# Attention and feed-forward kernel on one core: one of four chains of the first product of batches 2 to 5 written as one level of Strassen

## The chip, the core and the metric

The kernel runs on one core of a Trainium2 chip. The engines of the core are TensorE (PE in the profile, with PEld for the loading of its weights), VectorE (DVE), ScalarE (ACT), GpSimd (POOL) and SyncE (SP, which here only issues DMA transfers). Each engine works through its own list of instructions in the order in which the program wrote them, and waits on semaphores for the others. The metric is device time in microseconds (us); lower is better.

## The reference, cut to what matters

For 8 batches, 12 heads, 448 rows and 64 columns a head, the reference computes attention with normed q and k, and passes the result x (8 x 448 rows, 768 columns) through two matrix products with a leaky ReLU between them:

```python
q_n, k_n = rmsnorm(q, g_q), rmsnorm(k, g_k)
scores = 1/sqrt(64) * q_n @ k_n.T ; scores -= max ; attn = exp(scores) ; attn /= sum
x = (attn @ v) laid out as (3584, 768)
h = x @ w_in              # 768 -> 2048, the first product
g = maximum(0.01 * h, h)
out = g @ w_out           # 2048 -> 768, the second product
```

## The kernel before, in words

**Units.** The attention is cut into 24 units u of four heads each; three units make a batch (`NQ` is 3). In the main loop each unit has four quarters d = 0 to 3. In each quarter TensorE first makes the scores of one or two steps of keys (`qk`, L195; one step in quarter 0, two in the others, each into a slot of two PSUM banks, of which there are two). ScalarE takes the exponential of each slot (`ex`, L214), about 1 us a slot. In quarter 0 the unit also fixes its shift: VectorE takes the maximum of the first scores (`shift_max`, L232 and L234), TensorE spreads it with a matmul (`shift_mm`, L244), VectorE reduces once more (L245) and makes the bias `eb` (L253). Between the two, TensorE runs attention times v (`pv`, L340) and the row sums (`zcol`, L283) of the unit before. ScalarE copies the former out of PSUM (L295), SP spreads the reciprocal row sums (`rz`, L310), and GpSimd multiplies the two into the fp16 tile `xt` of the batch (L320).

**Preparation.** Two units ahead, q and k are normed: ScalarE squares them (`prep_sq`, L144, quarter 3), VectorE sums the squares (`prep_ssq`, L155, quarter 1), ScalarE makes the reciprocal root with a logarithm and an exponential (`prep_rinv`, `uu` on L160 and `rinv` on L161, quarter 2, written behind the exponentials of that quarter), VectorE multiplies (`prep_norm`, L167, once for q and once for k), and a transposing DMA on SP makes `qkT` (L179), which VectorE scales (`prep_g`, L151). The q and k tiles rotate through three buffers (`raws`), and unit u issues the loads of unit u + 4 in its quarter 0.

**The filling work.** The two products of a batch are cut into items, held in the list `queue`. `push(b)` adds those of batch b in quarter 3 of the first unit of batch b + 1, and `fill` (L702) takes some of them after the scores of each quarter, by a planned cost per item, so that they are spread over three units. A batch of the middle has 16 items of the first product, one for each of 16 row tiles of 128 hidden columns, called M here (`moe1`, L358): 6 matmuls of 448 columns into one PSUM bank, then one leaky ReLU by ScalarE (`prelu`, L356) into the fp16 tile `gt`. Then come the items of the second product: plain ones (`moe2`, L403) and groups of seven (`seven`, L444), a level of Strassen, with its operand sums on VectorE (`s1` to `s4`, L425 to L434). An even batch runs `moe2` for one tile and then one `seven`; an odd one runs two `seven`. The results go through the `ost` tiles (four buffers) to HBM on SP.

**What orders the work.** The program is written out under a manual schedule: each engine's order is the order in which the functions are called. A step of an item that reads its result (a copy, an addition, a ReLU) is put off with `later` and written at the head of the next item (`flush`). The jobs of a quarter (`jobs`) are written between its items, one after each. Four PSUM banks (`aux`) serve the items in rotation. `hold` takes all four into a list kept by the program, from which `aux` then takes the first and to which `drop` gives back.

**Where Strassen stands before.** Only batches 6 and 7 use it for the first product (`late1`, L552). A chain s covers four row tiles (2s, 2s + 1, 8 + 2s, 9 + 2s), and has seven items instead of four M: each has 6 matmuls of 224 columns (L564). Its operands are sums of weights (`win_sum`, L533) and sums of x (`x_sum`, L550); VectorE copies and adds the products in PSUM (L577, L583, L612) and ScalarE applies the ReLU (L574). Batch 6 has two chains beside 8 M, batch 7 has four. The weight sums of the second half of the tiles and the x sums of batch 6 are made in quarter 0 of unit 22.

Of the kernel before, what the change touches and what calls it, by code (L numbers as in the profile page):

```python
# [8 lines left out]
FP32 = mybir.dt.float32  # L9
# [9 lines left out]
def kernel(  # L19
# [47 lines left out]
    def drop(bank):  # L67
        if held:
            held[0].append(bank)

# [45 lines left out]

    def load(u, engines=None):
        raw[u] = [raws.tile([P, 2, NS, D], FP32, tag=name, name=name) for name in ("rq", "rk")]
        st[u] = {}
        for t, src, eng in zip(raw[u], (q, k), engines or (nc.sync, nc.sync)):  # L120
            eng.dma_start(t.rearrange("p a t d -> p a (t d)"), rows(src, u))
# [12 lines left out]
    def buf(u, name):  # L134
        if name not in st[u]:
            shape, dtype, bufs = SHAPES[name]
            st[u][name] = prep_p.tile(shape, dtype, tag=name[:2] if bufs == 3 and name != "qkT" else name, bufs=bufs, name=name)
        return st[u][name]
# [219 lines left out]
    def moe1(b, ft):  # L358
        xt = xts[b]
        hps = aux([P, 512], FP32, "hps")  # L360
        for kt in range(KT):
            nc.tensor.matmul(hps[:, 0:S], win16[:, kt // 2, kt % 2, ts(ft, P)], xt[:, kt // 2, kt % 2],  # L362
                             start=(kt == 0), stop=(kt == KT - 1))
        prelu(b, gt[:, ft, 64 * (b % 2):64 * (b % 2) + S], hps[:, 0:S])
        drop(hps)
# [157 lines left out]
    def win_sum(n, x, tile_=None, eng=nc.vector):  # L523
        if tile_ is None:
            ws[n, x] = win_b(1, 0, 4 * x, 4)
        else:
            pool, tag, bufs = tile_
            ws[n, x] = pool.tile([P, HK, 512], FP16, tag=tag, bufs=bufs, name="ws")
        a, b = {1: (lambda: (win_b(1, 0, 4 * x, 4), win_b(1, 1, 4 * x, 4))),
                2: (lambda: (ws[1, x], win_b(0, 0, 4 * x, 4))),  # L530
                3: (lambda: (win_b(0, 0, 4 * x, 4), win_b(1, 0, 4 * x, 4))),
                4: (lambda: (win_b(0, 1, 4 * x, 4), ws[2, x]))}[n]()
        eng.tensor_tensor(ws[n, x], a, b, op=ALU.add if n == 1 else ALU.subtract)  # L533
# [5 lines left out]
    def x_tiles():  # L539
        if not xs:  # L540
            two = [prep_p.tile([P, 2, HK, HX], FP16, tag="sq", bufs=3, name="xs") for i in range(2)]
            for n in range(1, 5):
                xs[n] = two[n // 3][:, (n - 1) % 2].rearrange("p k (t x) -> p k t x", t=NS)

    def x_sum(b, n):
        x_tiles()
        t = xs
        a, c = {1: (x_b(b, 0, 1), x_b(b, 0, 0)), 2: (x_b(b, 1, 1), t[1]),
                3: (x_b(b, 1, 1), x_b(b, 0, 1)), 4: (x_b(b, 1, 0), t[2])}[n]
        nc.vector.tensor_tensor(t[n], a, c, op=ALU.subtract)  # L550

    def late1(b, tail, after):  # L552
# [36 lines left out]
        def start():  # L589
            hold()  # L590
            if tail:
                for i in range(2):
                    drop(slot()[:, 0])
            for name in ("u", "v"):
                if name not in tmp:
                    tmp[name] = raws.tile([P, 2, S], FP32, tag="rq" if name == "u" else "rk", name=name)

        def item(n, s):
# [11 lines left out]
            elif n == 7:  # L610
                mm(get(7, s), 7, s, xs[3], True)
                later(lambda: nc.vector.tensor_copy(tmp["v"][:, s % 2], g[7, s][:, 0:S]))  # L612
            elif n == 6:
                mm(g[1, s], 6, s, xs[2], False)
                later(lambda: vadd(g[7, s][:, 0:S], g[1, s], tmp["v"][:, s % 2]))
            elif n == 5:
                mm(g[1, s], 5, s, xs[1], False)
                later(lambda: vadd(tmp["v"][:, s % 2], g[1, s], tmp["v"][:, s % 2]))
                later(lambda: out_(s, 1, 1, tmp["v"][:, s % 2]))
            elif n == 4:  # L620
                mm(g[7, s], 4, s, xs[4], False)
                later(lambda: out_(s, 1, 0, g[7, s][:, 0:S]))
                later(lambda: drop(g[7, s]))
            else:
                mm(g[1, s], 3, s, x_b(b, 1, 1), False)
                later(lambda: out_(s, 0, 1, g[1, s][:, 0:S]))
                later(lambda: drop(g[1, s]))
            for fn in after.get((n, s), ()):
                pend.append(fn)

        return item

    LATE_ALL = ((1, 0), (2, 0), (7, 0), (1, 1), (6, 0), (7, 1), (1, 2), (5, 0), (4, 0), (6, 1), (3, 0), (2, 1), (7, 2), (5, 1),
                (4, 1), (6, 2), (3, 1), (1, 3), (7, 3), (5, 2), (4, 2), (6, 3), (3, 2), (2, 2), (5, 3), (4, 3), (2, 3), (3, 3))
    LATE_HALF = ("M", "M", "M", "M", "M", "M", (1, 2), (7, 2), (2, 2), (6, 2), "M", (1, 3), (5, 2), (4, 2), (7, 3), (3, 2), (6, 3),
# [11 lines left out]
    def push(b):  # L647
# [7 lines left out]
        if late:  # L655
# [5 lines left out]
            else:  # L661
                after[6, 2] = [lambda: win_sum(1, 0, (raws, "rq", 3))]
                after[1, 3] = [lambda: win_sum(2, 0, (raws, "rk", 3))]
                after[5, 2] = [lambda: win_sum(4, 0, (prep_p, "n16", 1))]
            item = late1(b, odd, after)
            fts = [0, 8, 1, 9, 2, 10, 3, 11]
            items = []
            for w in (LATE_ALL if odd else LATE_HALF):
                if w == "M":
                    items.append((1.13, lambda ft=fts.pop(0): (flush(), moe1(b, ft))))  # L670
                else:
                    items.append((0.575, lambda w=w: item(*w)))
        if odd:
            tt, tn = (3, 4), (5, 6)
            items += [(1.31, fn) for fn in seven(pair, tt, tn)]
            for n, x, fs in ((len(items) - 7, 1, (s3, s4)),) if late else ((8, 0, (s1, s2)), (10, 0, (s3, s4)), (FT - 1, 1, (s1, s2)), (FT, 1, (s3, s4))):
# [67 lines left out]
    with tc.manual_schedule():  # L744
# [182 lines left out]
        for u in range(3, NU):  # L927
            for d in range(4):
# [24 lines left out]
                if d == 0:  # L953
# [8 lines left out]
                    if u + 4 < NU:  # L962
                        job(load, u + 4)
# [18 lines left out]
                if u + 2 < NU:  # L982
# [3 lines left out]
                    if d == 2:  # L986
# [3 lines left out]
                        if u > 3:  # L990
                            job(prep_trd, u + 2)
                if d == 1 and 4 <= u < 8:
# [3 lines left out]
                if d == 2 and 6 <= u < 8:  # L996
                    job(xmul_sb, u - 1)
                if u == NU - 2 and d == 0:
                    for n, tile_ in ((1, (raws, "rq", 3)), (2, (raws, "rk", 3)), (3, None), (4, (prep_p, "sq", 3))):
                        job(win_sum, n, 1, tile_)  # L1000
# [45 lines left out]
```

## Time and profile before

| | |
|---|---|
| median of 3 runs | 422.35 us (421.35 to 423.44) |
| profiled execution | 422.04 us, of which the span from first to last instruction is 420.3 us |
| PE busy | 404.4 us, 96% of the span |
| ACT busy | 303.6 us, 72% |
| DVE busy | 269.2 us, 64% |
| POOL busy | 83.0 us, 20% |
| first product, 448 columns (L362) | 600 matmul records, 120.8 us busy |
| its leaky ReLU (L356) | 100 instructions, 556 ns each |

Busy is the time in which an engine had an instruction running. Matmuls overlap in the records, so one lasts longer than the distance to the next; what a matmul costs is that distance. "Idle before" an instruction is the time for which its engine waited for it, with the releaser named behind an arrow. The middle stage, batches 2 to 5 in units 9 to 20, lies between about 143 us and 340 us.

### The profile page before, as it was taken

The numbers are of one execution on the slowest core, as the hardware profiler recorded it, in microseconds if no ns is written. First come the engines' busy times: TensorE is split into PE (matmuls) and PEld (weight loads), VectorE is DVE, ScalarE is ACT, GpSimd is POOL, SyncE is SP. The second block draws the span as 40 slices with busy tenths as digits, with TensorE's granted clock in tenths as the row PEclk, the third lists the DMA queues.
The fourth block names the chain that finished last, engine by engine and source line by source line (L and its number), as shares of the span: only waits on it lengthen the run. The fifth ranks groups of instructions, "written<-read, shape, count | busy, mean of one in ns | idle before, by whom it ended". The sixth has DMA issues, their size and how long they took to land.

```text
span 420.3 us, 9568 instructions
## 1 busy us (share of the span) xinstructions
PE 404.4 (96%) x3959; PEld 222.9 (53%) x3959; DVE 269.2 (64%) x440; ACT 303.6 (72%) x474; POOL 83.0 (20%) x75
## 2 busy tenths in 40 slices
PE   7977999999999999999999999999999999999995
PEld 6544444555445544555445544455445557558853
DVE  5788665787658736466448745467338787527762
ACT  5999878868987689867986779967986657653600
POOL 1958422300020111210121111120101101010000
PEclk9699999999999999999999999999999999999999
DMA  8999999889664795678565796578562460032023
GB/s 257 218 239 237 235 250 147 200 156 215 169 153 68 224 212 120 168 163 180 152 130 107 194 203 150 151 141 170 180 111 44 121 155 11 7 78 75 2 53 100
DMA packets 71951, 62.42 MB, mean 149 GB/s; under 512 B 36324, under 2 KB 67044, under 8 KB 71908
## 3 DMA queue, kind: packets, MB, share of 16 engines
q1 hardware_dynamic: 61312, 49.62, 47.2%
q0 software_dynamic: 10272, 11.80, 18.1%
q8 instruction: 31, 0.51, 0.5%
q10 hardware_dynamic: 324, 0.39, 0.3%
q14 instruction: 12, 0.10, 0.1%
HBM read 45.61 MB, written 11.01 MB: 135 GB/s over the span
## 4 chain that ended last, share of the span: by engine, by line
PE 83%; ACT 8%; DVE 6%; issue 1%; DMA 1%; SPq 0%; DVEq 0%; ACTq 0%
PE hps L362 27%; PE sT L195 8%; PE sT L340 6%; PE ma L444 5%; PE md L444 5%; PE mc L444 5%; ACT et L214 5%; PE bank L444 5%; PE bank L564 4%; PE op L403 3%; PE zc L283 3%; PE mb L444 3%; DVE n L167 2%; PE sT L444 2%; PE bank L403 1%
## 5 line engine op out<-in xcount | busy, mean ns | idle before, releaser
L214 ACT ACTIVATE et<-sT,eb 128x896 f16<-128x896 f32 x166 | 159.4, 1010 | 18.6 <-PE sT L195 16.9
L362 PE MATMUL hps<-xt,win 128*128 128x448 f16 x600 | 120.8, 353 | 0.2 <-DVE xt L349 0.2
L362 PEld LDWEIGHTS <-win 128*128 128x128 f16 x612 | 56.8, 98 | 58.2 <-issue 9.6
L320 POOL TENSOR_TENSOR xt<-x,rz 128x896 f16<-128x896 f32 x16 | 33.4, 2085 | 148.0 <-DMA rz<-zs 139.5
L356 ACT ACTIVATE gt<-hps 128x448 f16<-128x448 f32 x100 | 54.0, 556 | 6.1 <-PE hps L362 5.4
L167 DVE TENSOR_TENSOR n<-rq,rinv 128x896 f16<-128x896 f32 (+2 forms) x25 | 27.2, 1090 | 47.0 <-ACT rinv L161 44.2
L195 PE MATMUL sT<-qkT 64*64 64x448 f16 x664 | 53.2, 369 | 3.0 <-ACT et L214 1.9
L155 DVE TENSOR_REDUCE ssq<-sq 128x14 f32<-128x896 f32 (+2 forms) x49 | 50.3, 1058 | 1.6 <-ACT sq L144 1.6
L444 PEld LDWEIGHTS <-sa 128*128 128x128 f16 x352 | 32.8, 98 | 26.3 <-issue 6.1
L295 ACT COPY x<-sT 128x896 f32<-128x896 f32 x19 | 17.2, 906 | 36.4 <-DVE sT L245 36.4
L124 POOL DMA_DIRECT2D vt<-in_v_dram x24 | 18.2, 757 | 114.9 <-PE sT L340 107.4
L444 PEld LDWEIGHTS <-gt 128*128 128x128 f16 x264 | 25.2, 98 | 18.7 <-issue 2.1
L195 PEld LDWEIGHTS <-qkT 64*64 64x64 f16 x672 | 15.2, 105 | 36.8 <-issue 33.5
L340 PE MATMUL sT<-et,vt 64*64 64x448 f16 x532 | 28.5, 350 | 0.3
L403 PE MATMUL op<-wout,gt 128*128 128x384 f16 x160 | 28.4, 327 | 0.0
L232 DVE TENSOR_REDUCE sT<-sT 128x1 f32<-128x896 f32 x22 | 24.1, 1093 | 4.3 <-PE sT L195 4.3
L340 PEld LDWEIGHTS <-vt 64*64 64x64 f16 x672 | 20.7, 107 | 11.3 <-issue 1.7
L167 DVE TENSOR_TENSOR n<-rk,rinv 128x896 f16<-128x896 f32 (+2 forms) x26 | 26.1, 1009 | 0.0
L403 PEld LDWEIGHTS <-gt 128*128 128x128 f16 x192 | 17.6, 98 | 14.3 <-issue 3.0
L444 PE MATMUL ma<-wout,gt 128*128 128x384 f16 x128 | 23.5, 326 | 0.0
L425 DVE TENSOR_TENSOR sa<-gt 128x512 f16<-128x512 f16 (+1 forms) x15 | 8.2, 544 | 18.5 <-ACT gt L356 13.9
L144 ACT ACTIVATE sq<-rq 128x896 f32<-128x896 f32 (+2 forms) x18 | 16.3, 913 | 1.3 <-DMA rq<-in_q_dram 1.3
(135 smaller groups left out, 516.6 us busy)
## 6 DMA issues: line engine op xcount, KB each, us to landing
rq<-in_q_dram SPq DMA_DIRECT2D x24, 448.0 KB, 3.9
rk<-in_k_dram SPq DMA_DIRECT2D x24, 448.0 KB, 5.6
out_dram<-ost SPq DMA_DIRECT2D x52, 192.0 KB, 3.3
rz<-zs SPq DMA_DIRECT2D x76, 112.0 KB, 2.3
vt<-in_v_dram POOLq DMA_DIRECT2D x24, 224.0 KB, 5.1
win<-in_moe_w_in_dram POOLq DMA_DIRECT2D x8, 384.0 KB, 16.8
wout<-in_moe_w_out_dram POOLq DMA_DIRECT2D x2, 1536.0 KB, 29.7
out_dram<-ost SPq DMA_DIRECT2D x4, 96.0 KB, 2.1
```

The source lines that it names most:

```text
L124: nc.gpsimd.dma_start(vts[u % NV].rearrange("p a t d -> p a (t d)"), rows(v, u))
L155: nc.vector.tensor_reduce(buf(u, "ssq")[:, ti, :, c[0]:c[1]], buf(u, f"sq{ti}")[:, :, c[0]:c[1]], axis=AXL.X, op=ALU.add)
L167: nc.vector.tensor_tensor(buf(u, "n16")[:, ti, c[0]:c[1]].rearrange("p s a d -> p a s d"), src[:, :, c[0]:c[1]], buf(u, "rinv")[:, ti, :, ...
L195: nc.tensor.matmul(banks[a][64 * r:64 * r + 64, 0:S].rearrange("p (t x) -> p t x", t=NS), kT(u, r, a, t), qT(u, r, a), start=True, stop=True)
L214: nc.scalar.activation(s["et"][:, t], sT[:, :, 0:S], AF.Exp, bias=s["eb"], scale=1.0)
L232: nc.vector.tensor_reduce(s["spare"][:, 511:512], sT[:, :, 0:S], axis=AXL.XY, op=ALU.max)
L320: eng.tensor_tensor(xts[b][:, g], s["x32"], s["rz"], op=ALU.mult)
L340: nc.tensor.matmul(s["pv"][r][64 * a:64 * a + 64, 0:S], vts[u % NV][64 * r:64 * r + 64, a, t], s["et"][64 * r:64 * r + 64, t, a], start=(t ...
L356: nc.scalar.activation(dst, src, AF.Prelu, bias=0.0, scale=1.0, alpha=0.01)
L362: nc.tensor.matmul(hps[:, 0:S], win16[:, kt // 2, kt % 2, ts(ft, P)], xt[:, kt // 2, kt % 2], start=(kt == 0), stop=(kt == KT - 1))
L403: nc.tensor.matmul(op2[:, 0:HC], gt[:, ft, ds(col(t), P)], wout16[:, ft, ds(HC * half, HC)], start=(ft == 0), stop=(ft == FT - 1))
L444: nc.tensor.matmul(bank[:, 0:HC], a[:, f], b[:, f], start=(first and f == 0), stop=(f == HF - 1), skip_group_check=not first)
```

## The change

In batches 2 to 5 the chain s = 2 (row tiles 4, 5, 12 and 13) is computed by seven Strassen items instead of four M. The other twelve tiles stay M. The list `MID_HALF` sets the order of the 19 items; each is named by product and chain.

- The items of the chain are in the new function `mid`. It takes three banks: product 1 in one, product 7 in one, and a third that first gets a copy of product 1 by VectorE and in which products 6, 5 and 3 are then accumulated. That third bank is taken by `written`, from those whose 448 columns TensorE has written. Products 2 and 4 are accumulated on 1 and 7. VectorE makes a copy of 1, a copy of 7 into an `ost` tile `w`, and two additions; ScalarE makes four ReLUs of 448 columns.
- The four x sums of a batch are written as jobs in quarter 0 of its middle unit (units 10, 13, 16 and 19), behind the maximum, into two `ost` tiles.
- The weight sums of the upper half of the tiles are halved: their first 256 columns are made in unit 9, one in each quarter, and the rest in quarter 0 of unit 22.
- Buffers: q and k tiles and squares now rotate through two buffers from unit 9 on; the third holds the weight sums. From unit 7 on the loads of unit u + 4 are written in quarter 2, behind the transposing DMA, instead of in quarter 0.
- The banks are held in the program's list from batch 2 on, instead of from batch 6.
- The first halves of the sums `s1` to `s4` of an odd batch are written at items 14 and 15 (before: 8 and 10), the second halves at 18 and 19 (before: 15 and 16).

By the built program the order on the engines moves in these places: in unit 10 the VectorE order is now square sum, copy of 1, square sum, copy of 7, norm of q, first addition, norm of k, second addition (unit 16 alike); in unit 13 it is copy of 1, square sum, copy of 7, square sum, first addition, norm of q, norm of k, second addition (unit 19 alike). In unit 11 (and 17) TensorE's quarter 2 has one M and one `moe2` item and quarter 3 two `moe2` items (before: two M and one `moe2`, then one `moe2`), and VectorE has norm of q, `s1`, norm of k, the copy of `moe2`, `s2`, `s3`, `s4` and then the maximum of the next unit (before: both norms, `s1`, copy, `s2`, maximum, with `s3` and `s4` behind the bias). In unit 13 ScalarE's ReLU of `w` stands ahead of the two exponentials of quarter 3.

```diff
-    def drop(bank):
+    full = []
+    def drop(bank, whole=False):
         if held:
             held[0].append(bank)
+            full[:] = [x for x in full if x is not bank] + [bank] * whole
+    def written():
+        for i, x in enumerate(held[0]):
+            if any(x is y for y in full):
+                return held[0].pop(i)
...
+    def ring(pool, tag, third, shape, dtype, name):
+        return pool.tile(shape, dtype, tag=tag + "ab"[third], bufs=1 if third else 2, name=name)
...
-        raw[u] = [raws.tile([P, 2, NS, D], FP32, tag=name, name=name) for name in ("rq", "rk")]
+        raw[u] = [ring(raws, name, u in (2, 5, 8), [P, 2, NS, D], FP32, name) for name in ("rq", "rk")]
...
+        def mid(n, s):
+            flush()
+            hold()
+            if n == 1:
+                mm(get(1, s), 1, s, x_b(b, 0, 0), True)
+                later(lambda: g.__setitem__((6, s), written()))
+                later(lambda: nc.vector.tensor_copy(g[6, s][:, 0:S], g[1, s][:, 0:S]))
+            elif n == 7:
+                mm(get(7, s), 7, s, xs[b][3], True)
+                g["w", s] = opool.tile([P, S], FP32, tag="ost", name="w")
+                later(lambda: nc.vector.tensor_copy(g["w", s], g[7, s][:, 0:S]))
+            elif n == 2:
+                mm(g[1, s], 2, s, x_b(b, 1, 0), False)
+                later(lambda: out_(s, 0, 0, g[1, s][:, 0:S]))
+                later(lambda: drop(g[1, s], True))
+            elif n == 6:
+                mm(g[6, s], 6, s, xs[b][2], False)
+                later(lambda: vadd(g[7, s][:, 0:S], g[6, s], g["w", s]))
+            elif n == 5:
+                mm(g[6, s], 5, s, xs[b][1], False)
+                later(lambda: vadd(g["w", s], g[6, s], g["w", s]))
+                later(lambda: out_(s, 1, 1, g["w", s]))
+            elif n == 4:
+                mm(g[7, s], 4, s, xs[b][4], False)
+                later(lambda: out_(s, 1, 0, g[7, s][:, 0:S]))
+                later(lambda: drop(g[7, s], True))
+            else:
+                mm(g[6, s], 3, s, x_b(b, 1, 1), False)
+                later(lambda: out_(s, 0, 1, g[6, s][:, 0:S]))
+                later(lambda: drop(g[6, s], True))
...
+    MID = 2
+    MID_HALF = ("M", "M", "M", (1, 2), (7, 2), "M", (2, 2), (6, 2), "M", (5, 2), (4, 2), "M", (3, 2), "M", "M", "M", "M", "M", "M")
...
-            item = late1(b, odd, after)
-            fts = [0, 8, 1, 9, 2, 10, 3, 11]
+        if b >= MID:
+            item = late1(b, late and odd, after)
+            fts = [0, 8, 1, 9, 2, 10, 3, 11, 6, 14, 7, 15]
...
-                    if u + 4 < NU:
+                    if u + 4 < NU and u < 7:
                         job(load, u + 4)
...
                         if u > 3:
                             job(prep_trd, u + 2)
+                        if u + 4 < NU and u >= 7:
+                            job(load, u + 4)
...
+                if u == 3 * MID + 3:
+                    n, tile_ = ((1, (raws, "rqb", 1)), (2, (raws, "rkb", 1)), (4, (prep_p, "sqb", 1)), (3, None))[d]
+                    job(win_sum, n, 1, tile_, 0)
+                if d == 0 and u % NQ == 1 and MID < u // NQ <= LATE:
+                    for n in (3, 1, 2, 4):
+                        job(x_sum, u // NQ - 1, n)
```

## The prediction

> **What bounds the kernel now.** I read the page's slices, then busy time by stretch, then the timelines of units 10 and 12, then the chain of waits for the rate of matmuls.
>
> ```profile
> PE   7977999999999999999999999999999999999995
> ...
> DVE  5788665787658736466448745467338787527762
> ACT  5999878868987689867986779967986657653600
> ```
>
> ```profile
> 150.00:175.00 25.00, 25.00 (x213) 11.74 (x212) 10.51 (x14) 23.32 (x41) 4.90 (x3) 1.00 0.71 169
> 200.00:225.00 25.00, 25.00 (x211) 12.29 (x210) 13.27 (x23) 21.26 (x36) 4.94 (x3) 1.00 0.55 133
> ```
>
> The columns: stretch, length, busy time of PE, PEld, DVE, ACT, POOL, then clock and DMA. TensorE has no gap in the middle stage: a matmul removed there is worth its full time, a wait put there costs its full time. VectorE is half idle, but the average does not say when it reaches an instruction. Its order does (unit 10, third quarter):
>
> ```profile
> 155.34 2.44 PE L362 MATMUL hps<-xt,win 128*128 128x448 f16 x12
> 155.39 1.90 ACT L214 ACTIVATE et<-sT,eb 128x896 f16<-128x896 f32 x2
> ...
> 157.16 0.55 ACT L356 ACTIVATE gt<-hps 128x448 f16<-128x448 f32 x1
> 157.59 0.34 ACT L160 ACTIVATE uu<-ssq,eps_t 128x28 f32<-128x28 f32 x1
> ...
> 157.96 0.23 ACT L161 ACTIVATE rinv<-uu 128x28 f32<-128x28 f32 x1
> ...
> 158.21 1.48 DVE L167 TENSOR_TENSOR n<-rq,rinv 128x896 f16<-128x896 f32 x1 [6.63 <-ACT rinv L161]
> ```
>
> VectorE stands 6.63 us before the norm of q, for a root that ScalarE makes behind two exponentials. Whatever is written on VectorE behind that norm waits too; before, nothing for TensorE stood there. And the border to unit 12, the maximum and the matmul that needs it:
>
> ```profile
> 176.04 1.52 PE L340 MATMUL sT<-et,vt 64*64 64x448 f16 x28
> ...
> 176.74 1.09 DVE L232 TENSOR_REDUCE sT<-sT 128x1 f32<-128x896 f32 x1
> ...
> 177.86 0.29 DVE L234 TENSOR_TENSOR dg<-ident,sT 128x128 f16<-128x128 f16 x1
> ...
> 178.27 0.23 PE L244 MATMUL sT<-dg,onesp 128*128 128x64 f16 x2
> ```
>
> The operand `dg` is ready at 178.15 and used at 178.27: about 0.1 us of slack.
>
> [...] in the timeline 12 of 448 columns and the step to the scores take 2.38 us (155.34 to 157.72), and in the chain of waits 12 of 224 take 1.15 us, 96 ns each. [...] in the built program products 5 and 3 do wait for VectorE.
>
> **The change part by part.** F is the time at which a quarter's filling items start, after its scores.
>
> *Matmuls.* A batch gives up 24 of 448 columns (24 x 0.1885 = 4.52 us) and gets 42 of 224 (42 x 0.096 = 4.03). Gain 0.49, four batches: **-1.97 us**, all on the path. ReLUs: four of 448 columns for four, no change.
>
> *VectorE work added.* Per batch four x sums (0.50 us each by their row, 2.0), copies and additions (0.62 each; PSUM to PSUM has no row, I bound it by 0.54, the copy of 384 columns, and 0.65, just above the PSUM addition of 0.63). The sums stand behind `eb`; the 6.63 us idle cover them and the copies. The square sums get later, but the second ends 3.6 us after the second quarter's F, 2.4 us before ScalarE asks for it. Without that cover it would be up to 2 us a batch. The weight sums (half of a 0.95 us row, about 0.5 each) are only moved; in unit 22 they stood under an M-filled quarter, so I count no gain.
>
> *First addition, units 10 and 16.* The root: 158.21 - 155.34 = 2.87 after F, minus 0.43 (157.16 to 157.59) since no ReLU stands ahead of it now: 2.44. The norm of q takes 1.01 from start to start in the undisturbed units, the addition 0.62: done at F + 4.1. Product 5 overwrites the bank that the addition reads. TensorE asks for it after products 2 and 6 (1.15), an M (1.13) and the scores (0.6): F + 2.9. Wait 1.2. Also, the second quarter's first and last item share a bank: its ReLU stands behind two exponentials, 0.1 more. Queued behind on TensorE: everything. Bounds 0.8 (short norm) to 2.1 (norm at its 1.48 us, bank wait 0.45). **2 x 1.36 = +2.7 us**.
>
> *Second addition, units 13 and 19.* Here it follows both norms: 2.45 + 1.01 + 1.0 + 0.62 = F + 5.1. Product 3 is asked for after products 6, 5, 4 (1.73), M (1.13), the scores (0.6), M (1.13): F + 4.6. Wait 0.5. And the ReLU of `w` waits for it ahead of the last two exponentials on ScalarE: ReLU, ReLU of product 4 (0.43 each), two exponentials (1.9) end at F + 7.9, where attention times v would have been reached at F + 6.6. Together 1.3; then ScalarE catches up by the next bias (its work before the copy of x adds up to 2.9 us, the bias comes at 2.9). Bounds 0.8 to 2.0. **2 x 1.3 = +2.6 us**.
>
> *The maximum of units 12 and 18.* Two `moe2` items now lie ahead of the border, so `s3` and `s4` (0.6 us each from start to start) come before the maximum, less 0.2 that the copy waited: it is 1.0 later against 0.1 of slack, while TensorE arrives as before. I take 1.0 (bounds 0.5 to 1.5): **+2.0 us**. In return the longer fourth quarter covers the exponentials for which `pv` waited there (scores end 175.77, `pv` 176.04; alike in 18): **-0.5 us**.
>
> *The border to unit 10.* One `seven` item (1.3 us) slips from unit 9 to 10. `pv` then waits 0.3 for the exponentials; the maximum, behind a norm, two weight sums and an addition, starts at 146.4 and ends with `dg` at 147.85, where TensorE comes at 147.4. Bounds 0.2 to 1.1: **+0.8 us**.
>
> *The loads of q and k, and the buffers.* Per unit two loads (448 KB, 3.8 and 4.7 us to landing) pass behind the transposing DMA on SP and still ahead of the next unit's `rz`; GpSimd's queue is not changed. Both wait for the same norm. The squares come some 14 us after the new issue: cost nothing. If `rz` comes later by them, xt has some 6 us left (done at 187.9, first used at 194.46), else up to 1 us a batch. `w` and the x tiles wait for stores that were issued half a unit before: nothing.
>
> Sum: -1.97 - 0.5 + 2.7 + 2.6 + 2.0 + 0.8 = **+5.6 us**. The profiled execution would go from 422.04 (span 420.3) to 427.6; it is 0.3 below the median of 422.35, from which I get 427.9. I say 427.8.
>
> **The rivals.**
> 1. *The additions come in time: faster.* If the first addition is done by F + 2.9 and the maximum isn't late, only the gains are left: 422.35 - 2.5 = 419.9. For it: the chains of batch 6, interleaved with scores in the same way, run without a gap from 348.6 to 356.2. Against: there no norm stands in VectorE's order. It decides at 1.2 us: so much earlier the root would have to come. 11%.
> 2. *The waits are at their low ends.* Lower bounds 0.8, 0.8, 0.5 (twice each) and 0.2 give 4.4, less 2.5: 424.2. For it: a wait lets VectorE and ScalarE catch up, and two waits in neighbouring units can be one. Against: the units named are mostly not neighbours in cause. 13% that it ends within 0.5%.
> 3. *ScalarE becomes the bound.* It is 93% busy with M items; if the 2.2 us that it stands for `w` are not made good within a unit, 1 to 1.5 us come on top in each of units 14 and 20, and half in 11 and 17: about 431. For it: little slack. Against: work before the next bias just fits. 10%.
> 4. *The change does not do what it says*: 224-column matmuls bound by their weight loads (98 ns each) would lose 0.08 us a batch, which changes nothing.
>
> **How the numbers follow.** Forecast (slower, 425 to 430.5) 66%, with 427.8 the likeliest; rivals 11%, 13% and 10%. 0.5%, 2.1 us, is about what a measurement of this kernel can tell from no change. Faster 0.11, same 0.13, slower 0.76. The range goes from the low ends (424.2) up to 430.8, short of both extremes at once.
>
> **What would show it.** TensorE's records in 150 to 340 us would show idle time released by VectorE before products 5 (units 10, 16) and 3 (13, 19), by ScalarE before `pv` (14, 20), by VectorE before the spread of the maximum (10, 12, 18), together some 7 to 8 us; matmuls of L586 at 96 ns. If VectorE's idle time before the norm of q no longer ends with the root, or product 5 starts right behind the scores, the forecast is wrong.

## The result, and the profile after

| | before | after |
|---|---|---|
| median | 421.33 us (420.84 to 423.44, 6 runs) | 436.82 us (435.89 to 440.15, 6 runs) |
| profiled execution, its span | 422.04, 420.3 us | 437.06, 435.3 us |
| PE busy | 404.4 us (96%) | 405.4 us (93%) |
| DVE busy | 269.2 us | 293.1 us |

The ratio is 1.0368, 95% interval 1.0328 to 1.0409. The forecast was 5.6 us more; it is 15.5 us more. The sign was right, the size was not. Here are the slices of the page after, TensorE's row and its granted clock:

```profile
PE   8787999999999979999899998999789999999996
PEclk9999999999999988999999999999999999999999
```

TensorE is no longer at 9 from end to end in the middle, and there are two slices at 8 in the clock row, of which the forecast says nothing (in that row of before only the second slice is below 9, at 6). The same by stretches (the last two columns are the DMA engines' busy share and GB/s):

```profile
150.00:175.00 25.00, 22.24 (x191) 12.08 (x190) 13.93 (x19) 17.48 (x30) 2.83 (x2) 0.86 0.63 163
200.00:225.00 25.00, 23.75 (x248) 13.35 (x241) 14.27 (x27) 20.20 (x34) 4.55 (x3) 1.00 0.76 181
250.00:275.00 25.00, 23.44 (x242) 13.44 (x239) 14.40 (x24) 20.19 (x34) 3.58 (x3) 1.00 0.82 192
300.00:325.00 25.00, 19.92 (x199) 11.54 (x188) 13.35 (x21) 17.14 (x29) 3.32 (x3) 1.00 0.72 175
```

Before, these stretches had 25.00, 25.00, 24.90 and 25.00. They hold units 10, 13, 16 and 19, those with a chain. What TensorE waited for between 140 and 345 us, where the kernel before has no line at all (columns: total, times, longest):

```profile
PE bank L586 <- DVE bank L599: 7.6, 4, 2.8
PE sT L259 <- DVE dg L249: 3.1, 4, 1.0
PE bank L586 <- DVE w L599: 1.5, 1, 1.5
PE sT L355 <- ACT et L229: 1.0, 2, 0.5
PE bank L459 <- DVE ost L466: 0.4, 1, 0.4
```

(In the kernel after, L586 is the chain's matmul, L599 its additions, L663 the copy of product 7 into `w`, L182 the norm, L335 GpSimd's multiply, L249 to L259 the shift's operand and its spread, L355 `pv`, L133 the loads of q and k, L325 `rz`, L397 the output stores.) Half of it is the first addition, and it waits in all four units, not in two. Unit 10, third quarter, answers to the lines shown of before:

```profile
153.73 1.74 SPq L397 DMA_DIRECT2D out_dram<-ost  x2
...
156.61 0.62 DVE L663 COPY w<-bank 128x448 f32<-128x448 f32 x1 [1.46 <-DMA out_dram<-ost]
...
157.82 2.07 POOL L335 TENSOR_TENSOR xt<-x,rz 128x896 f16<-128x896 f32 x1 [10.92 <-ACT et L229]
...
158.14 2.69 DVE L182 TENSOR_TENSOR n<-rq,rinv 128x896 f16<-128x896 f32 x1 [0.91 <-ACT rinv L176]
...
160.76 0.62 DVE L599 TENSOR_TENSOR bank<-bank,w 128x448 f32<-128x448 f32 x1
...
161.43 1.28 PE L586 MATMUL bank<-xs,ws 128*128 128x224 f16 x6 [2.76 <-DVE bank L599]
...
163.63 2.44 PE L377 MATMUL bank<-xt,win 128*128 128x448 f16 x6
```

Two things are new here. The norm of q takes 2.69 us; it took 1.48 in this unit before, and 1.09 where nothing ran beside it. It starts 0.32 us after GpSimd's multiply and ends 0.94 us after its end (157.82 + 2.07 = 159.89). (The view puts the multiply's own wait down to an exponential; its input `rz`, issued from 150.5 to 152.7 us, landed 4.9 to 6.2 us later.) And behind the 2.76 us idle, six matmuls of 448 columns take 2.44 us instead of 1.30: half rate. In unit 19 the first addition is late for another reason:

```profile
299.83 1.10 SPq L133 DMA_DIRECT2D rq<-in_q_dram  x1
300.98 0.48 SPq L133 DMA_DIRECT2D rk<-in_k_dram  x1
301.58 3.03 SPq L397 DMA_DIRECT2D out_dram<-ost  x4
304.72 5.43 SPq L325 DMA_DIRECT2D rz<-zs  x4
...
310.39 0.62 DVE L663 COPY w<-bank 128x448 f32<-128x448 f32 x1 [3.19 <-DMA out_dram<-ost]
...
311.93 0.62 DVE L599 TENSOR_TENSOR bank<-bank,w 128x448 f32<-128x448 f32 x1
...
312.60 0.74 PE L586 MATMUL bank<-xs,ws 128*128 128x224 f16 x6 [2.51 <-DVE bank L599]
312.65 2.93 DVE L182 TENSOR_TENSOR n<-rq,rinv 128x896 f16<-128x896 f32 x1
```

The copy of product 7 stands 3.19 us for its tile: `w` is one of the four `ost` tiles, and an output store still reads it. The stores were issued right behind the two loads that the change moved, and took 7.6 to 8.2 us to land.

My theory was then: the matmuls do gain 2.0 us; the loss is waits of TensorE, and they come (a) from stores that hold `w`, (b) from norms on VectorE that last longer beside GpSimd's multiply (2.69 and 2.93 us instead of 1.09), (c) from VectorE's order, as forecast, and (d) a long wait can cost again through the clock, as the 2.44 us instead of 1.30 behind that of 2.76 us. Rivals: the root on ScalarE alone makes the additions late; VectorE or ScalarE is too full, whatever the order.

### The profile page after: what moved, and what is told of

The parts are those of the page before. It is cut to its first block, busy times and chain, and to the rows that moved or that the text cites. A ratio compares the mean times of both kernels' runs of the same rounds, so it can differ in the third digit from the quotient of the medians.

```text
span 435.3 us, 9756 instructions
## 1 busy us (share of the span) xinstructions
PE 405.4 (93%) x4031; PEld 231.1 (53%) x4031; DVE 293.1 (67%) x476; ACT 304.7 (70%) x474; POOL 84.1 (19%) x75
## 4 chain that ended last, share of the span: by engine, by line
PE 64%; ACT 12%; DVE 12%; issue 5%; DMA 4%; SPq 1%; DVEq 0%; ACTq 0%
PE bank L459 16%; PE bank L377 10%; PE hps L377 8%; ACT et L229 7%; PE bank L586 6%; PE sT L210 6%; PE sT L355 5%; DMA out_dram<-ost 3%; DVE n L182 3%; PE bank L418 2%; PE bank L298 2%; PE op L418 2%; PE sT L459 1%; DVE sT L247 1%; ACT gt L371 1%
## 5 line engine op out<-in xcount | busy, mean ns | idle before, releaser
L229 ACT ACTIVATE et<-sT,eb 128x896 f16<-128x896 f32 x166 | 159.4, 1009 | 14.6 <-PE sT L210 12.5
L377 PEld LDWEIGHTS <-win 128*128 128x128 f16 x516 | 48.5, 98 | 46.9 <-issue 7.8
L377 PE MATMUL bank<-xt,win 128*128 128x448 f16 x336 | 70.4, 357 | 0.0
L335 POOL TENSOR_TENSOR xt<-x,rz 128x896 f16<-128x896 f32 x16 | 34.5, 2155 | 163.4 <-DMA rz<-zs 152.4
L182 DVE TENSOR_TENSOR n<-rq,rinv 128x896 f16<-128x896 f32 (+2 forms) x25 | 31.1, 1246 | 30.8 <-ACT rinv L176 27.8
L377 PE MATMUL hps<-xt,win 128*128 128x448 f16 x180 | 36.6, 353 | 0.2 <-DVE xt L364 0.2
L210 PEld LDWEIGHTS <-qkT 64*64 64x64 f16 x672 | 15.5, 104 | 37.4 <-issue 34.1
L459 PE MATMUL bank<-tw,sa 128*128 128x384 f16 x192 | 34.2, 327 | 0.0
L371 ACT ACTIVATE gt<-bank 128x448 f16<-128x448 f32 x56 | 29.8, 554 | 6.3 <-PE bank L377 6.0
L466 DVE TENSOR_TENSOR ost<-bank,ost 128x384 f32<-128x384 f32 x40 | 22.1, 553 | 14.4 <-PE bank L459 12.4
L355 PE MATMUL sT<-et,vt 64*64 64x448 f16 x532 | 29.0, 354 | 1.2 <-ACT et L229 1.0
L355 PEld LDWEIGHTS <-vt 64*64 64x64 f16 x672 | 21.1, 108 | 12.8 <-issue 3.6
L182 DVE TENSOR_TENSOR n<-rk,rinv 128x896 f16<-128x896 f32 (+2 forms) x26 | 27.5, 1065 | 0.0
L459 PE MATMUL bank<-wout,gt 128*128 128x384 f16 x144 | 26.6, 327 | 0.2 <-ACT gt L596 0.2
```

What stands on the lines that cost most here:

```text
L182: nc.vector.tensor_tensor(buf(u, "n16")[:, ti, c[0]:c[1]].rearrange("p s a d -> p a s d"), src[:, :, c[0]:c[1]], buf(u, "rinv")[:, ti, :, ...
L210: nc.tensor.matmul(banks[a][64 * r:64 * r + 64, 0:S].rearrange("p (t x) -> p t x", t=NS), kT(u, r, a, t), qT(u, r, a), start=True, stop=True)
L229: nc.scalar.activation(s["et"][:, t], sT[:, :, 0:S], AF.Exp, bias=s["eb"], scale=1.0)
L335: eng.tensor_tensor(xts[b][:, g], s["x32"], s["rz"], op=ALU.mult)
L355: nc.tensor.matmul(s["pv"][r][64 * a:64 * a + 64, 0:S], vts[u % NV][64 * r:64 * r + 64, a, t], s["et"][64 * r:64 * r + 64, t, a], start=(t ...
L371: nc.scalar.activation(dst, src, AF.Prelu, bias=0.0, scale=1.0, alpha=0.01)
```

## The experiments

All edits are to the kernel after. Line numbers in e1, e6 and e9 are one higher.

**e1, `w` in a tile of its own** (tests a).

```diff
+    wpool = ctx.enter_context(tc.tile_pool(name="wpool", bufs=1))
...
-                g["w", s] = opool.tile([P, S], FP32, tag="ost", name="w")
+                g["w", s] = wpool.tile([P, S], FP16, tag="w", name="w")
```

> The copy of product 7 gets a tile of its own (fp16) instead of one of the four output tiles, so that it no longer waits for output stores. Theory (stores delay VectorE): VectorE's waits of 1.5, 1.4 and 3.2 us before that copy go; in the unit with the 3.2 us (unit 19) the root and the first addition come about 2 us earlier, in unit 13 about 0.8; in unit 10 the norm is late for other reasons and stays. Total about 2.5 us less than the changed kernel: 434.3 us. Rival (the first addition is late because of the root on ScalarE and the norm alone, as predicted): no difference, 436.8.

Measured: 433.84 us, ratio 1.0292 (1.0255 to 1.0330). The copy waits for no store any more, and by the medians 3.0 us are won, near the 2.5 expected. But the trace does not bear that size out: the profiled execution is the slowest of the four (436.33 us), and in it TensorE's waits fall only from 13.6 to 12.8 us. The path is other than I wrote, too: the first addition waits in units 10 (2.61) and 16 (2.32) only, as forecast, and the second in unit 19 for 2.22 us. (a) is a part of it; how large a part is not shown here.

**e2, norms a quarter later** in units 10, 13, 16 and 19, with the transposing DMA and the loads behind them.

```diff
                     if d == 2:
                         job(prep_rinv, u + 2)
+                    if d == (3 if u in (10, 13, 16, 19) else 2):
                         for ti in range(2):
                             job(prep_norm, u + 2, ALL, (ti,))
```

> In units 10, 13, 16 and 19 the two norms, their transposing DMA and the loads behind it are written a quarter later, so that both additions stand on VectorE ahead of the norms. Theory: the first addition waits for the norm of q (in units 10 and 16) and through it for GpSimd's multiply; TensorE's 2.8 and 1.6 us before product 5 go, those of unit 19 shrink, and the 3 us of half clock behind the 2.8 us idle go too: 436.8 - 2.8 - 1.6 - 3.0 = 429.4, give or take 1.5. Rival (the additions are late because VectorE has too much to do in these units, whatever the order): over 434.

Measured: 431.25 us, ratio 1.0220 (1.0171 to 1.0268), just above what was expected (429.4, give or take 1.5). The first addition waits in units 13 and 19 alone; unit 19 shows the wait for the store without any norm in front:

```profile
306.25 0.62 DVE L663 COPY w<-bank 128x448 f32<-128x448 f32 x1 [3.49 <-DMA out_dram<-ost]
...
308.46 0.73 PE L586 MATMUL bank<-xs,ws 128*128 128x224 f16 x6 [2.82 <-DVE bank L599]
```

The price is at the maximum (5.9 us at `dg` instead of 3.1, 1.73 to 1.78 in units 10, 12 and 18).

**e3, `s3` and `s4` behind the maximum** in batches 2 and 4 (tests the term of 2.0 us).

```diff
-                std[2] = also(std[2], lambda: later(s3, tt), lambda: later(s4, tt))
+                n = 3 if MID <= b < LATE else 2
+                std[n] = also(std[n], lambda: later(s3, tt), lambda: later(s4, tt))
```

> In batches 2 and 4 the sums s3 and s4 are written at the fourth plain item of the second product instead of the third, so that they stand behind the maximum of units 12 and 18. Theory: TensorE's 0.98 us before the spread of the maximum in both units go: 436.8 - 2.0 = 434.8 (435.5 if the seven that needs the sums then waits for them). Rival (the maximum is late for another reason): 436.8.

Measured: 434.70 us, ratio 1.0327 (1.0258 to 1.0396). The two waits of 0.98 us in units 12 and 18 are gone. The interval overlaps that of the kernel after, so the time alone would not carry it; the trace does. That the median moves by the 2.0 us expected is in part luck: in the trace other waits grow (unit 10's at the maximum from 0.71 to 1.72 us), so that their sum falls by 0.6 us only, and 1.7 us less are lost by the clock.

**e4, the wait in unit 10 filled** (tests d).

```diff
             elif n == 5:
+                if b == 2:
+                    warm(40, held[0][0])
                 mm(g[6, s], 5, s, xs[b][1], False)
```

> In unit 10 alone, 40 matmuls of 128 columns whose result nothing reads are put on TensorE between product 4's predecessor and product 5, that is into its idle 2.76 us (they take some 2.2 us). Theory (the idle time costs a second time, since TensorE's clock is halved for 6 us behind it): the matmuls of 161 to 168 us run at full rate again and the time falls by about 3 us to 434. Rival (the half rate there has nothing to do with the idle time): 436.8 or more.

Measured: 438.54 us, ratio 1.0389 (1.0354 to 1.0423): a miss in time. In unit 10 the half clock is gone, but in this execution it stands behind two other waits, in unit 13 (idle 2.67 us, then clock 0.73 and 0.50) and unit 16. The first fence is of the kernel after, the second of e4:

```profile
160.00:162.00 2.00, 0.57 (x4) 0.45 (x4) 2.00 (x3) 1.61 (x2) 0.00 (x0) 0.65 0.00 0
162.00:164.00 2.00, 2.00 (x11) 1.42 (x10) 0.99 (x2) 0.59 (x2) 0.00 (x0) 0.50 0.18 35
164.00:166.00 2.00, 2.00 (x6) 0.59 (x5) 0.00 (x0) 1.25 (x2) 0.00 (x0) 0.50 1.14 206
166.00:168.00 2.00, 2.00 (x29) 1.06 (x32) 1.25 (x2) 0.54 (x1) 0.00 (x0) 0.64 0.95 267
```

```profile
160.00:162.00 2.00, 1.67 (x29) 1.55 (x27) 2.00 (x3) 1.99 (x3) 0.17 (x1) 1.00 0.00 0
162.00:164.00 2.00, 2.00 (x17) 1.35 (x14) 1.18 (x2) 0.78 (x2) 0.00 (x0) 1.00 0.06 12
...
210.00:212.00 2.00, 1.32 (x9) 1.10 (x9) 1.90 (x3) 0.98 (x3) 1.49 (x1) 0.73 0.00 0
212.00:214.00 2.00, 2.00 (x14) 0.68 (x13) 2.00 (x2) 0.00 (x0) 0.58 (x1) 0.50 0.00 0
```

So the loss by the clock came with waits of this length, but not with a certain one; more on this below.

**e5, loads behind `rz`** (tests a and b at their common source).

```diff
+                    if u + 3 < NU and u >= 8:
+                        job(load, u + 3)
...
-                        if u + 4 < NU and u >= 7:
-                            job(load, u + 4)
```

> From unit 8 on, the loads of q and k are written in quarter 0 of the next unit, behind the spread of the reciprocal row sums, instead of in quarter 2, so that output stores and that spread stand ahead of them on SP. Theory: the copy of product 7 no longer waits for stores that stand behind loads (1.5, 1.4 and 3.2 us in units 10, 13, 19) and GpSimd's multiply is done before the norm of q starts, which takes 1.1 us again instead of 2.2 to 2.9. TensorE's waits for the first addition fall from 7.6 to about 4 us: 433 us, give or take 1.5. Rival (the additions are late because of the root on ScalarE alone): 436 to 437.

Measured: 429.77 us, ratio 1.0184 (1.0169 to 1.0199), more than expected. One edit to the order on SP takes off 7 of the 15 us. Unit 10 of e5:

```profile
151.14 3.26 SPq L325 DMA_DIRECT2D rz<-zs  x4
154.50 1.19 SPq L397 DMA_DIRECT2D out_dram<-ost  x2
155.70 0.62 DVE L663 COPY w<-bank 128x448 f32<-128x448 f32 x1
155.73 0.60 SPq L133 DMA_DIRECT2D rq<-in_q_dram  x1
156.26 2.07 POOL L335 TENSOR_TENSOR xt<-x,rz 128x896 f16<-128x896 f32 x1 [9.47 <-DMA rz<-zs]
...
158.77 1.09 DVE L182 TENSOR_TENSOR n<-rq,rinv 128x896 f16<-128x896 f32 x1 [2.45 <-ACT rinv L176]
159.78 0.63 DVE L599 TENSOR_TENSOR bank<-bank,w 128x448 f32<-128x448 f32 x1
...
160.45 0.73 PE L586 MATMUL bank<-xs,ws 128*128 128x224 f16 x6 [1.16 <-DVE bank L599]
```

No wait for a store; the multiply ends before the norm begins; the norm takes 1.09 us, and the wait is 1.16 us, against 1.2 in the forecast; in unit 16 it is the same. Not every unit is clear of it: in unit 19 the norm of q still meets a multiply and takes 2.17 us, and the second addition waits 1.42 us.

**e6, the four edits e1, e2, e3 and e5 together** (can the chain pay at all?).

> All of it: own fp16 tile for the copy of product 7, norms of units 10, 13, 16 and 19 a quarter later, s3 and s4 behind the maximum, loads behind the spread of the row sums. Theory (the loss is waits of TensorE that the order on VectorE and SP makes, and no longer idle time, so no half clock): of about 14 us of waits and half clock some 2 us are left (the border to unit 10, attention times v): 424, between 421 and 427. Rival (a chain costs more than it saves however the rest is ordered, because VectorE or ScalarE is too full): over 428.

Measured: 421.57 us, ratio 0.9988 (0.9972 to 1.0004), at the low end of the expectation. TensorE's waits in the middle are 1.5 us in all. VectorE and ScalarE are not too full.

**e7, buffers only**: plain tiles as before, the rest of the change stays. The weight sums of unit 9 overwrite weights that plain tiles 12 and 13 use, so the output is not the reference's.

```diff
-        if b >= MID:
+        if MID <= b < LATE:
+            items = [(1.13, lambda ft=ft: (flush(), hold(), moe1(b, ft))) for ft in order]
+        elif late:
             item = late1(b, late and odd, after)
...
```

> Batches 2 to 5 keep their sixteen tiles in plain form in the order of the kernel before; no chain, no x sums, sums of the second product where they were. Left of the change: two buffers instead of three, loads in quarter 2, banks held in the program's list, halved weight sums in unit 9. Theory: on their own they cost next to nothing, since nothing for TensorE stands behind the store or the norm that become late: the kernel before plus 0 to 1 us, 422.6. Rival (moved loads or buffers cost by themselves): 425 or more.

Measured: 425.11 us, ratio 1.0070 (1.0043 to 1.0096). The rival was right: without any chain, 3 us are lost. Of TensorE's waits in this trace, 5.6 us, late maxima are 4.9. In unit 11 it is a norm ahead of the maximum that takes 2.97 us:

```profile
173.56 1.09 DVE L182 TENSOR_TENSOR n<-rq,rinv 128x896 f16<-128x896 f32 x1 [2.32 <-ACT rinv L176]
173.92 2.67 POOL L335 TENSOR_TENSOR xt<-x,rz 128x896 f16<-128x896 f32 x1 [10.37 <-DMA rz<-zs]
...
174.56 2.97 DVE L182 TENSOR_TENSOR n<-rk,rinv 128x896 f16<-128x896 f32 x1
...
179.13 1.08 DVE L247 TENSOR_REDUCE sT<-sT 128x1 f32<-128x896 f32 x1
...
180.59 0.22 PE L259 MATMUL sT<-dg,onesp 128*128 128x64 f16 x2 [1.54 <-DVE dg L249]
```

It goes both ways: GpSimd's multiply, begun inside the norm of q, takes 2.67 instead of 2.07 us, and the norm of k, begun inside the multiply, ends 0.94 us after it.

**e8, no copies and no additions** on VectorE; products 6, 5 and 3 go into a fresh bank, and the fourth ReLU reads product 7's bank.

```diff
-                later(lambda: g.__setitem__((6, s), written()))
-                later(lambda: nc.vector.tensor_copy(g[6, s][:, 0:S], g[1, s][:, 0:S]))
...
-                mm(g[6, s], 6, s, xs[b][2], False)
-                later(lambda: vadd(g[7, s][:, 0:S], g[6, s], g["w", s]))
+                mm(get(6, s), 6, s, xs[b][2], True)
...
```

> The chain's matmuls, its four leaky ReLUs and the x sums stay, but VectorE's two copies and two additions a batch are left out (products 6, 5 and 3 are gathered in a fresh bank, and the fourth ReLU reads product 7's bank), so that the output is not the reference's. Theory: only the gain of the matmuls is left, less the waits at the border to units 10, 12 and 18: the kernel before - 2.0 - 0.5 + 2.0 + 0.7 = 422.5. Rival (ScalarE's ReLUs or the held banks make the loss, not the additions): over 428.

Measured: 425.35 us, ratio 1.0092 (1.0066 to 1.0119), 2.9 us over the expectation and short of the rival. TensorE waits for no chain; what is left is again the maximum (3.6 us, up to 1.83 in unit 12) and 1.0 us for an `ost` tile. It bounds the cost of the copies and additions: 436.82 - 425.35 = 11.5 us with all that hangs on them.

**e9, e6 with the weight sums of unit 9 in quarters 0 and 1.**

```diff
-                if u == 3 * MID + 3:
-                    n, tile_ = ((1, (raws, "rqb", 1)), (2, (raws, "rkb", 1)), (4, (prep_p, "sqb", 1)), (3, None))[d]
-                    job(win_sum, n, 1, tile_, 0)
+                if u == 3 * MID + 3 and d < 2:
+                    four = ((1, (raws, "rqb", 1)), (2, (raws, "rkb", 1)), (4, (prep_p, "sqb", 1)), (3, None))
+                    for n, tile_ in (four[1:] if d else four[:1]):
+                        job(win_sum, n, 1, tile_, 0)
```

> The kernel with all four edits, and the last two of the four half weight sums of unit 9 written in quarter 1 beside the second instead of in quarters 2 and 3, so that none stands ahead of the maximum of unit 10. Theory: the 0.75 us before the spread of the maximum in unit 10 goes, of TensorE's waits in the middle stage 0.5 us is left, and the gain of the matmuls shows: 421.6 - 0.75 = 420.8, ratio to before about 0.997. Rival (the maximum of unit 10 is late because of the norms): 421.6, no change.

Measured: 421.15 us (22 runs) against 421.96 (43 runs) of the kernel before: ratio 0.9971 (0.9958 to 0.9985), the only version that beats it, by a little. The wait in unit 10 is 0.34 us instead of 0.75. TensorE has no gap in three of the stretches shown above:

```profile
150.00:175.00 25.00, 25.00 (x234) 13.58 (x232) 13.68 (x21) 22.82 (x39) 4.91 (x3) 1.00 0.71 177
200.00:225.00 25.00, 25.00 (x232) 13.60 (x234) 17.50 (x28) 21.95 (x37) 4.90 (x3) 1.00 0.53 133
300.00:325.00 25.00, 25.00 (x260) 13.18 (x260) 17.98 (x32) 20.47 (x32) 3.23 (x3) 1.00 0.52 103
```

**e10, e7 with the loads behind `rz`** (the edit of e5).

> The kernel with buffers only (plain tiles, no chain; the weight sums of unit 9 overwrite weights that plain tiles 12 and 13 use, so that the output is not the reference's, as in the run before), but with the loads written behind the spread of the row sums. Theory (the 3 us of the buffers come from the loads ahead of that spread on SP: GpSimd's multiply comes later, runs into the norms[...]): 422.3, no norm over 2.2 us in units 11 and 17. Rival (two buffers instead of three, or the held banks): 425 again.

Measured: 422.42 us, ratio 1.0001 (0.9988 to 1.0013). As expected: with the loads behind `rz` the loss of e7 is no longer told from none, so its cause is the place of the loads on SP, not the two buffers or the held banks. The same norms in e10:

```profile
171.98 2.07 POOL L335 TENSOR_TENSOR xt<-x,rz 128x896 f16<-128x896 f32 x1 [7.55 <-DMA rz<-zs]
```

```profile
173.90 1.11 DVE L182 TENSOR_TENSOR n<-rq,rinv 128x896 f16<-128x896 f32 x1 [5.09 <-ACT rinv L176]
174.93 1.08 DVE L182 TENSOR_TENSOR n<-rk,rinv 128x896 f16<-128x896 f32 x1
```

**e11, GpSimd's multiply written two quarters later** (meant to test b alone).

```diff
-                if d == 1 and narrow(u - 1) and not 5 <= u < 8 and u < NU - 1:
+                if d == (3 if u in (10, 13, 16, 19) else 1) and narrow(u - 1) and not 5 <= u < 8 and u < NU - 1:
```

> The changed kernel with one edit: GpSimd's multiply of units 10, 13, 16 and 19 is written two quarters later, behind the norms; loads, stores and the copy's tile stay. Theory [...]: the norms of q in units 10, 16 and 19 take 1.1 us instead of 2.7, 1.5 and 2.9, the first addition comes as much earlier, and without an idle time of over 2 us there is less half clock: 436.8 - 1.6 - 0.4 - 1.8 - 2 to 3 = about 430.5, between 429 and 432.5, and the copy of product 7 still waits for stores. Rival (the norm is long for another reason, or the stores alone make the addition late): over 434.

Measured: 436.33 us, ratio 1.0335 (1.0292 to 1.0379): no change, and no verdict on b, since the edit moved nothing. The multiply of unit 10 starts at 158.62, about when its last input has landed (`rz`, issued from 151.4 to 153.3 us, takes 5.1 to 6.2 us); GpSimd has nothing else ahead of it, so the place in the program does not matter.

**e12, that multiply on VectorE**, in quarter 3 of the same four units (b alone).

```diff
+                if d == 3 and u in (10, 13, 16, 19):
+                    job(xmul_sb, u - 1)
-                if d == 1 and narrow(u - 1) and not 5 <= u < 8 and u < NU - 1:
+                elif d == 1 and narrow(u - 1) and not 5 <= u < 8 and u < NU - 1 and u not in (10, 13, 16, 19):
```

> The edit before this one (multiply written later) did not move the multiply, since GpSimd has nothing ahead of it and starts it when the row sums land. Here the multiply of units 10, 13, 16 and 19 is taken from GpSimd and put on VectorE behind the norm of k, in quarter 3; loads, stores and the copy's tile stay as in the changed kernel. Theory [...]: the norms of q in units 10, 16 and 19 take 1.1 us; TensorE's waits for the first addition in units 10 and 16 fall to about 1.15 us each (from 2.7 and 1.6), the one for the second addition in unit 19 (1.5) goes, that for the first in unit 19 (2.5) stays since it comes from the store: 436.8 - 3.5, less 1 to 2 of half clock: 431.8, between 430 and 434. Rival (the norms are long for another reason): 436 or more, as VectorE gets 4 us more.

Measured: 431.13 us, ratio 1.0213 (1.0165 to 1.0261). Loads, stores and `w` are where they were, VectorE even has 4 us more to do, and 5.7 us are won. Unit 10:

```profile
159.09 1.09 DVE L182 TENSOR_TENSOR n<-rq,rinv 128x896 f16<-128x896 f32 x1 [1.97 <-ACT rinv L176]
160.10 0.62 DVE L599 TENSOR_TENSOR bank<-bank,w 128x448 f32<-128x448 f32 x1
...
160.78 0.73 PE L586 MATMUL bank<-xs,ws 128*128 128x224 f16 x6 [1.16 <-DVE bank L599]
```

The wait is 1.16 us in unit 10 and in unit 16, the 1.15 expected. In unit 19, where 2.5 us were to stay, it is 1.78, with the copy still waiting 2.45 us for a store; in unit 13 it is 1.31. TensorE's waits fall by 2.7 us in all (13.6 to 10.9); the other 3.4 us between the two profiled spans are half clock that this execution doesn't have.

**All of them in one sum.** If the theory holds, each span is 420.3 (before), less 2.0 where there is a chain, plus TensorE's waits between 140 and 345 us (all lines of that view), plus the loss by the clock there (one minus the granted clock, summed over stretches of 1 us). Half clock in the first 40 us, which some of these traces have, that of before among them (3.4 us by the same measure, between 11 and 19 us), is left out. For e4 the 40 added matmuls are counted too (they start from 159.0 to 161.2 us, 2.2).

| kernel | waits | clock | sum | span |
|---|---|---|---|---|
| after | 13.6 | 3.4 | 435.3 | 435.3 |
| e1 | 12.8 | 3.4 | 434.5 | 434.6 |
| e2 | 9.6 | 1.7 | 429.6 | 430.2 |
| e3 | 13.0 | 1.7 | 433.0 | 433.3 |
| e4 | 13.3 | 3.4 | 437.2 | 437.2 |
| e5 | 9.3 | 0 | 427.6 | 428.1 |
| e6 | 1.5 | 0 | 419.8 | 419.4 |
| e7 (no chain) | 5.6 | 0 | 425.9 | 425.0 |
| e8 | 4.6 | 0 | 422.9 | 421.8 |
| e9 | 1.1 | 0 | 419.4 | 418.8 |
| e10 (no chain) | 0.9 | 0 | 421.2 | 421.3 |
| e11 | 12.5 | 1.7 | 432.5 | 433.2 |
| e12 | 10.9 | 0 | 429.2 | 429.2 |

Thirteen spans over a range of 18 us come out within 1.1 us. Nothing of size is left for a rival such as slower matmuls. The sum is a balance: it shows where the time of an execution lies, not why a wait is there. The spans are of single executions; the device times of these are up to 2.5 us away from the medians, since a wait or a loss by the clock falls a little differently each time.

## Why the prediction was wrong

Right were the place and the kind of the loss (waits of TensorE for VectorE at products 5 and 3 and at the maximum), the gain and several terms. The size failed, by three steps: the stores that hold `w`, the later `rz`, and the clock, each put at nothing or not put at all.

| step of the sum | predicted | in the trace after |
|---|---|---|
| matmuls | -2.0 | -2.0: product 6 and the M behind it start 0.58 us apart (156.29, 156.87), 96 ns a matmul; before, 24 of 448 columns took 4.54 us (from 340.16 us on), 189 ns each; the table above closes with it |
| first addition, units 10 and 16 | +2.7 | 2.76 + 1.56 = 4.3 |
| first addition, units 13 and 19 | 0 | 0.76 + 2.51 = 3.3 |
| second addition, units 13 and 19 | +2.6 | 0 + 1.51, and `pv` 2 x 0.5: 2.5 |
| maximum, units 12 and 18 | +2.0 | 2 x 0.98 |
| border to unit 10 | +0.8 | 0.71 |
| `pv` of units 12 and 18 covered | -0.5 | not seen; the view of waits of before has no such line |
| not in the forecast: border in unit 19, an `ost` tile | 0 | 0.47 + 0.37 |
| not in the forecast: half clock | 0 | 3.4 |

The right column gives -2.0 + 4.3 + 3.3 + 2.5 + 2.0 + 0.7 + 0.8 + 3.4 = 15.0, the difference of the spans (435.3 - 420.3) of the two profiled executions. Two slips of the prediction are small beside that: its first addition has 1.2 + 0.1 us and is summed as 1.36, and it gives its range as 425 to 430.5 and as 424.2 to 430.8.

**"`w` and the x tiles wait for stores that were issued half a unit before: nothing."** This failed for `w`. The prediction took the stores at the place that they had before. But it had itself moved two loads of 448 KB ahead of them on SP. In unit 19 the stores land 7.6 to 8.2 us after their issue (5.0 to 6.2 in e5), the tile comes free at 310.4, 3.19 us after VectorE was there, and product 5 waits 2.51 us; in units 10 and 13 the copy waits 1.46 and 1.44 us. e1 takes the tile away from the stores, and no such wait remains; e5 puts the stores ahead of the loads, and none remains either.

**"If `rz` comes later by them, xt has some 6 us left."** The step asked who needs the product of GpSimd's multiply, and not what the multiply does to its neighbour while it runs. And `rz` came later without being issued later: in unit 10 its issues start from 150.5 to 152.7 us (before: 151.9 to 153.8), but behind the loads they take 5.7 us to land in the median, against 3.3 before and 3.1 in e5. What the multiply does to a norm that begins inside it can be read from the traces: in the kernel after the norms of q begun inside a multiply take 2.69, 2.15, 1.49 and 2.93 us, which is the rest of the multiply (1.75, 1.21, 0.55, 1.98) and 0.94 or 0.95 more; the others of that stage take 1.08 or 1.09. The trace of before had it as well, in the line of 158.21 that the prediction shows: 1.48 us, and the multiply of that unit is

```profile
156.66 2.08 POOL L320 TENSOR_TENSOR xt<-x,rz 128x896 f16<-128x896 f32 x1 [7.91 <-DMA rz<-zs]
```

It ends at 158.74, 0.53 us after the norm began: 0.53 + 0.95 = 1.48. The forecast took 1.48 as the upper end of a spread, "(norm at its 1.48 us ...)"; it was one point of this series, whose end I estimate from the same durations at 2.07 + 0.95 = 3.0 us; the norm of k in e7 took 2.97. With the multiply off GpSimd (e12), or early (e5), the wait in units 10 and 16 is 1.16 us: the step's own 1.2 us was right for an undisturbed norm. The excess over it is the norm's to the digit: 1.16 + (2.69 - 1.09) = 2.76 us in unit 10 and 1.16 + (1.49 - 1.09) = 1.56 in unit 16, the two waits of the kernel after. In these units of e1, e3 and e11, and in unit 16 of e4, where the norm takes 1.48 to 2.65 us, the same sum gives the wait to 0.01 us, seven times more. That the moved loads cost without a chain, too, is shown by e7 and e10: 3.1 and 0.5 us over before by the medians, where e10 is not told from no change.

**The clock was not in the sum at all.** The prediction treated a wait as costing its length. It can cost more: 3.4 us here, at half clock behind the first wait of 2.76 us. That a filled wait in unit 10 takes the half clock away there is shown by e4; that the time did not fall with it is as plain. How much of the 15.5 us of the medians is the clock stays open, for the 3.4 us are of one execution: of the six of the kernel after, one has a mean granted clock of 0.999, so that it lost some 0.4 us by it (0.001 x 434.1), and took 435.89 us, only 1.2 less than the profiled one with 0.990.

The second addition shows how a right total can rest on a shifted split: predicted was 0.5 at product 3 in both units and 0.8 behind it; it was 0 and 1.51, and 0.5 each at `pv`. The 1.51 is the norm of 2.93 us again: in e12, where that norm takes 1.09 us, no wait for `w` is listed.

Of the rivals none held: the additions were not in time; the waits were not at their low ends; ScalarE did not become the bound (`pv` waits 2 x 0.5 us, and nothing is listed in units 11 and 17); and the 224-column matmuls run at 96 ns.

What stays open: how the 7 us of e5 divide between stores and multiply in each unit. e1 (3.0 us) and e12 (5.7 us) each take one away, but each also shifts where the others fall, and in e12 the clock's share goes with them.

## What to carry to other kernels

When a change moves a transfer on a queue, follow every transfer that it passes to its landing, not only to its issue, and on to its last consumer: to the tile that a store frees, and to the engine that its landing starts. An instruction that sets off on another engine is not free for its neighbours merely because its result is early (here a norm took up to 2.97 us instead of 1.09 beside one): look at what runs beside it, and treat a duration that stands out in the profile (1.48 beside 1.09 us) as a rule to be found, not as noise. And where TensorE has no gap, a short gain at it is paid only if every engine that now stands between two of its matmuls is early: here the same 2.0 us of gain gave 3.7% slower or 0.3% faster, by the order of the work and one tile of its own.

## What the runs showed of the hardware that I had not expected

**Waits of TensorE of 1.89 us and more were followed by half clock in eight cases of thirteen.** In the traces of the thirteen kernels after the change there are 13 idle times of TensorE of 1.89 to 2.82 us in the middle stage. Eight were followed by half clock (2.76, 2.32, 2.22, 2.82, 2.00, 2.67, 1.89 and 2.57 us), five were not (2.51, 2.61, 2.46, 2.10 and 2.72). Of 17 between 1.4 and 1.83 us none was. The loss came in steps of about 1.7 us: in e3 the clock was 0.69, 0.50, 0.50 and 0.60 in the four stretches of 1 us from 162 to 166 us (0.31 + 0.50 + 0.50 + 0.40 = 1.71), and once, in the kernel after, two steps came together (the windows of 160 to 168 us above: 2 x (0.35 + 0.50 + 0.50 + 0.36) = 3.42). Which of two waits of like length is followed by half clock changes from kernel to kernel: 2.51 us in unit 19 of the kernel after was not, 2.57 us there in e11 was. What decides it no run here shows.

**A norm on VectorE and the multiply on GpSimd lengthened each other**: the multiply took 2.67 instead of 2.07 us when a norm had begun first (e7), and 3.03 in unit 13 of the kernel after, where it began 0.02 us after a norm; the norms begun inside a multiply took up to 2.97 us instead of 1.09 (e7).
